# Spreading transfers and moving the weight scaling in a fused attention and mixture-of-experts kernel

## The chip, the core and the metric

The kernel runs on one core of a Trainium2 chip. A core has a matrix engine (TensorE, PE in the rows), a vector engine (VectorE, DVE), a scalar engine (ScalarE, ACT), a general engine (GpSimd, POOL), a queue engine that issues transfers (SyncE, SP), and 16 DMA engines that move data between the device memory, called DRAM in the code, and the on-chip memory. Matmul results land in eight banks of a separate accumulator memory (PSUM). The metric is the device time of one execution in microseconds, the median of three runs.

## What is computed

For each of four batches, 12288 queries of 128 numbers attend to 768 keys. Keys and values are the same rows: a 4x4 mean over `kv`, times `w_sr`. Each attention output goes to one of eight experts, the one with the largest logit, and is scaled by two gates. Softmax and expert choice are per row, so no row waits for another.

```python
kv_pool = kv.reshape(B, H // r, r, W // r, r, C).mean(axis=(2, 4))
k = v = kv_pool.reshape(B, -1, C) @ w_sr
s = scale * (q @ k.transpose(0, 2, 1))
a = softmax(s)
x = a @ v                                   # 49152 rows of 128
e = argmax(x @ w_gate)
out = prob(e) * sigmoid(x @ w_output_gate)[e] * (relu(x @ w1[e]) @ w2[e])
```

## The kernel before

**Tiles.** 512 queries are a group (i, 96 of them, 24 a batch); four groups are a chunk (c, 24 of them). fp32 values are split into a high and a low half of fp16, and a product takes three matmuls (high x high, high x low, low x high). A chunk's most frequent expert is computed in place for all rows of the chunk; rows that chose another expert are written into per-expert lists and done at the end (`tail_tile`).

**Order.** The order of all engines is written out by hand. The outer loop runs over i, the inner one over eight steps s, and a letter string (`ORD`, in the first nine groups `ORDA`) gives the order of the parts in a step: `s` scores of a block of 128 queries (L375 to L379) with the row maximum nm (L381, L382), `h` the first expert product H (L697) with its halves HH (ScalarE, L702) and HL (VectorE, L703), `x` the exponential pr (L396), `r` the rounding of pr to ph (ScalarE L409, then GpSimd subtracts the low half, L410), `u` the product p v (L432: 18 matmuls in a row, at step 5), `y` the second expert product Y (L713 to L715), `e` events put off to a given step, `f` a piece of routing. While group i is at its scores, p v is at i - 1, the logits at i - 2, and the experts at i - 9 (`MOE_LAG`). So the first nine groups do attention alone. ph is transposed by DMA into PT (L415), which p v reads.

**VectorE, ScalarE and GpSimd run their own instructions in order.** A piece that waits holds everything behind it on its engine. H has three PSUM buffers, shared with U of p v.

**Routing.** `routing` (L488 to L603) works in pieces between yields: the sums sume (L499), the one-hot rows, the counts (L524, matmuls hung on the PSUM tile of a score block through `hooks`), the chunk's expert ei (L545), the gate product z (L555), msc, the list places idx (L583), the running list ends (nd and ebase, L586 to L588), and 16 scatters (L599), which wait until the lists are filled.

**Weights.** When the expert is known, `w_load` reads its w1 and w2 (1 MB). `w_split` measures them (L628, two reductions), spreads the two maxima over the rows (wmb L634, a transpose L639, L151 to L157), scales with GpSimd (L666), makes the high half on ScalarE (L673) and the low half on GpSimd (L679). msw (L656) holds the chunk's output factors.

**Transfers on the queue of SyncE.** Queries two groups ahead, keys of the next batch (24 loads of 256 KB, from group 9 of the first batch and group 3 of the others, one a step while at most two blocks are open), list fills (8 of 400 KB, `fill`, from group 9 on), attention values of each group (`u_turn`, a DMA transpose, and `u_out`, the store to `urows`; those of groups 0 to 5 are put off by 48 steps), expert weights and outputs. `kv_prep` sums four rows on GpSimd (L240 to L244), transposes (L248) and multiplies (L211) each of a batch's six key blocks.

Of the kernel before, what the change touches and what calls it, by code (L numbers as in the profile page):

```python
# [53 lines left out]
class Cfg:  # L54
# [8 lines left out]
    ORDA = "hsxruye"  # L63
# [6 lines left out]
    FS = 3  # L70
    HJ = (0, 1)
    H0 = (6, 0)
    LC = 4
    WD = 6
# [6 lines left out]
    UD = 6  # L81
    MT, MO = 4, 2
    KV0, KD = 9, 8
# [4 lines left out]
def body(ctx, tc, q, kv, w_sr, w_gate, w_og, w1, w2, out, cfg=Cfg):  # L88
# [54 lines left out]
    dve.memset(run.rearrange("p (e b) -> p e b", e=E)[:, :, 0:1], 0.0)  # L143
    prow = cst.tile([P, 1], I32, name="prow")
# [35 lines left out]
    KVN = [[0, 0] for _ in range(NB)]  # L180

    def kv_load(b, first=False):

        src = kv[b].rearrange("(ho hl rh) (wq w x) c -> ho w rh hl wq (x c)", ho=3, rh=4, wq=4, w=2)
        for k in range(NKB):
# [13 lines left out]
            for rh in range(4):  # L199
                sp.dma_start(out=halves[rh // 2][:, rh % 2, :], in_=src[k // 2, k % 2, rh])  # L200
                KVN[b][0] += 1
                yield

    def kv_prep(b, fast):
# [13 lines left out]
        for k in range(NKB):  # L218
            while KVN[b][0] < 4 * (k + 1):
# [31 lines left out]
            act.activation(pT, ps[:, 0, 0:P], AF.Copy, scale=1.0 / 16.0)  # L251
            yield
# [59 lines left out]
    def q_power(c, a, b):  # L312

        m, r = (QM[c][:, n, a:b] for n in range(2))
        dve.tensor_scalar(m, m, 2.0 ** -100, 2.0 ** -13, op0=ALU.max, op1=ALU.mult)
# [4 lines left out]
    def q_factor(c, a=0, b=CG):  # L320

        dve.tensor_scalar(QM[c][:, 2, a:b], QM[c][:, 0, a:b], KVT[c // NCH][2], None, op0=ALU.mult)
# [32 lines left out]
    hooks, now = [], [0]  # L355
# [71 lines left out]
    def pv(i, lo, hi, cols=slice(0, GT)):  # L427
# [5 lines left out]
        if hi == len(ops) and cols.stop == GT:  # L433
            u = PVP.pop(i)
            U2 = wk.tile([P, 2, GT], F16, tag="U2", bufs=MOE_LAG, name=f"U2{i}")
# [53 lines left out]
    def routing(c):  # L489
# [9 lines left out]
        dve.tensor_scalar(sume, SUM, vs[:, 0:1], vs[:, 1:2], op0=ALU.mult, op1=ALU.add)  # L499
# [64 lines left out]
        dve.tensor_scalar(sel, m2, cm[:, 1:2], None, op0=ALU.is_equal)  # L564
# [21 lines left out]
        dve.tensor_scalar(nd, w8, cm[:, 1:2], None, op0=ALU.not_equal)  # L586
        dve.tensor_tensor(nd, nd, cnt[:, 0, :], op=ALU.mult)
# [35 lines left out]
    def w_split(c, att):  # L623
        t = WT[c]
        m = kvp.tile([P, 7], F32, tag="wm", name=f"wm{c}")
        mb = kvp.tile([P, 2, P], F32, tag="wmb", bufs=1, name=f"wmb{c}")
        for n in range(2):
            dve.tensor_reduce(out=m[:, n:n + 1], in_=t[:, n, :], op=ALU.max, axis=AX.X,  # L628
                              apply_absolute_value=True)
            if n == 0:  # L630
                yield
                if att and c:
                    yield
        dve.tensor_copy(mb, m[:, 0:2].unsqueeze(2).to_broadcast([P, 2, P]))  # L634
# [7 lines left out]
        if att:  # L642
            hooks.append((now[0] + 2, turn))
        else:
            yield
            yield
# [3 lines left out]
        largest(m[:, 0:2], ps[0][:, :, 384:512])  # L650
# [461 lines left out]
```

## Time and profile before

| | us |
|---|---|
| median of three runs | 2066.92 (2061.56 to 2070.02) |
| profiled execution: its own time | 2066.82 |
| its span, first to last instruction | 2065.1 |
| TensorE busy | 1920.7 (93%) |
| VectorE busy | 1673.5 (81%) |
| GpSimd busy | 1367.5 (66%) |
| ScalarE busy | 1355.9 (66%) |
| mean granted TensorE clock | 0.983 |

The table holds averages over stages that differ: nine groups of attention alone until about 151 us, then groups with experts, with key preparation for the next batch until about 1330 us, and at the end the last expert groups with the lists. A busy share does not say who is late; the waits do. The rows further down are from one profiled execution. Matmuls overlap, so their mean duration is longer than the distance between them.

### The profile page before, as it was taken

The page shows a single profiled execution, that of the slowest core. Times are in us where ns is not written, and L with a number is a line of the kernel's source. Part 1 is how long each engine was busy: PE and PEld are TensorE (multiplying, and loading weights), DVE is VectorE, ACT ScalarE, POOL GpSimd, SP SyncE. Part 2 cuts the span into 40 slices and gives each one's busy share as a digit, 9 for nine tenths or more (in the row PEclk, how much of TensorE's full clock was granted, in tenths as well). Part 3 has the DMA queues.
Part 4 walks back from the last instruction along what each step waited for, and adds up shares of the span by engine and source line. Part 5 has one row for each costly group of instructions (what it writes and reads, how often), then busy time and mean ns, then how long its engine had stood idle before and what let it go on. Part 6 is the DMA issues. An engine that isn't in the chain of part 4 may idle for free.

```text
span 2065.1 us, 31969 instructions
## 1 busy us (share of the span) xinstructions
PE 1920.7 (93%) x10401; PEld 969.2 (47%) x10401; DVE 1673.5 (81%) x3277; ACT 1355.9 (66%) x2501; POOL 1367.5 (66%) x1111
## 2 busy tenths in 40 slices
PE   6878899899999999999999999999999999999996
PEld 4544444444444444444444444444444444444444
DVE  4777688888888888788888888888888888888773
ACT  2656666667677676666766776777777677667542
POOL 2554578788687687675776867856756857757431
PEclk8989999999999999999999999999999999999998
DMA  5959997878988877968889888788788788687411
GB/s 174 184 124 235 199 209 150 180 153 157 203 165 182 197 152 154 176 140 173 163 192 179 186 162 191 136 174 171 138 171 170 146 167 171 141 159 150 100 56 45
DMA packets 902199, 334.10 MB, mean 162 GB/s; under 512 B 820672, under 2 KB 849473, under 8 KB 902032
## 3 DMA queue, kind: packets, MB, share of 16 engines
q1 hardware_dynamic: 889120, 331.59, 77.0%
q0 software_dynamic: 12480, 0.40, 0.5%
q8 instruction: 82, 1.34, 0.3%
q14 instruction: 85, 0.70, 0.1%
q10 hardware_dynamic: 432, 0.07, 0.0%
HBM read 77.80 MB, written 54.53 MB: 64 GB/s over the span
## 4 chain that ended last, share of the span: by engine, by line
DVE 41%; PE 29%; ACT 12%; issue 11%; DMA 4%; POOL 2%; SPq 1%; ACTq 0%; DVEq 0%; POOLq 0%
DVE nm L381 9%; PE U L432 7%; DVE HL L703 7%; ACT pr L396 5%; ACT HH L702 4%; DVE wm L628 2%; PE Y L713 2%; DVE nm L382 2%; PE H L697 2%; PE H L698 2%; PE H L699 2%; PE Y L715 2%; PE Y L714 2%; DVE q L332 2%; DVE U L437 2%
## 5 line engine op out<-in xcount | busy, mean ns | idle before, releaser
L410 POOL TENSOR_TENSOR ph<-pr,ph 128x768 f16<-128x768 f32 x384 | 635.4, 1655 | 486.1 <-ACT ph L409 271.9
L703 DVE SCALAR_TENSOR_TENSOR HL<-H,HH 128x512 f16<-128x512 f32 x768 | 525.2, 685 | 112.6 <-ACT HH L702 102.7
L396 ACT ACTIVATE pr<-S,nm,qm 128x768 f32<-128x768 f32 x384 | 380.3, 990 | 316.8 <-DVE nm L382 287.8
L702 ACT ACTIVATE HH<-H 128x512 f16<-128x512 f32 x768 | 454.2, 592 | 182.4 <-PE H L699 179.3
L599 POOL DMA_INDIRECT scr<-rw,idx x384 | 385.6, 1004 | 97.6 <-issue 87.8
L432 PE MATMUL U<-PT,V 128*128 128x512 f16 (+1 forms) x1872 | 395.3, 366 | 23.2 <-DMA PT<-ph 13.7
L381 DVE TENSOR_REDUCE nm<-S 128x1 f32<-128x768 f32 x384 | 364.1, 948 | 37.5 <-PE S L379 37.3
L697 PE MATMUL H<-U,w 128*128 128x512 f16 x768 | 292.3, 381 | 35.9 <-DVE HL L703 34.1
L409 ACT ACTIVATE ph<-pr 128x768 f16<-128x768 f32 x366 | 307.6, 840 | 7.9 <-DMA PT<-ph 6.0
L713 PE MATMUL Y<-HH,w 128*128 128x512 f16 x768 | 292.9, 381 | 9.2 <-ACT ys L718 9.2
L714 PE MATMUL Y<-HH,w 128*128 128x512 f16 x768 | 291.6, 380 | 1.3 <-POOL w L679 1.3
L699 PE MATMUL H<-U,w 128*128 128x512 f16 x768 | 292.5, 381 | 0.0
L698 PE MATMUL H<-U,w 128*128 128x512 f16 x768 | 292.5, 381 | 0.0
L715 PE MATMUL Y<-HL,w 128*128 128x512 f16 x768 | 291.6, 380 | 0.3 <-DVE HL L703 0.3
L432 PEld LDWEIGHTS <-V 128*128 128x128 f16 x1872 | 184.1, 99 | 222.4 <-issue 25.3
L375 PE MATMUL S<-K,qT 128*128 128x384 f16 x768 | 190.6, 330 | 15.0 <-ACT pr L396 12.4
L379 PE MATMUL S<-K,qT 128*128 128x384 f16 x768 | 191.1, 331 | 0.0
L377 PE MATMUL S<-K,qT 128*128 128x384 f16 x768 | 190.9, 331 | 0.0
L733 DVE TENSOR_TENSOR o<-S,msw 128x256 f32<-128x256 f32 x172 | 73.0, 424 | 101.1 <-ACT pr L396 92.6
L698 PEld LDWEIGHTS <-w 128*128 128x128 f16 x768 | 75.2, 98 | 114.2 <-issue 55.3
L666 POOL TENSOR_SCALAR wr<-wr,wm 128x1024 f32<-128x1024 f32 x44 | 125.1, 2844 | 0.0
L714 PEld LDWEIGHTS <-w 128*128 128x128 f16 x768 | 75.4, 98 | 96.0 <-issue 20.1
(202 smaller groups left out, 2321.3 us busy)
## 6 DMA issues: line engine op xcount, KB each, us to landing
kvs<-in_kv_dram SPq DMA_DIRECT2D x96, 256.0 KB
q<-in_q_dram SPq DMA_DIRECT2D x96, 256.0 KB
wr<-in_moe_w_dram SPq DMA_DIRECT2D x48, 512.0 KB
urows<-uT SPq DMA_DIRECT2D x96, 256.0 KB
out_dram<-o SPq DMA_DIRECT2D x96, 256.0 KB
PT<-ph SPq DMA_TRANSPOSE x384
scr<-rw,idx POOLq DMA_INDIRECT x384
scr<-fill SPq DMA_DIRECT2D x8, 400.0 KB
```

Of the source, the lines that this page charges most:

```text
L381: dve.tensor_reduce(out=nm[:, 0:1], in_=S[:, :, 0:384], op=ALU.max, axis=AX.XY, negate=True)
L396: act.activation(pr.rearrange("p (a k) -> p a k", a=2), S[:, :, 0:384], AF.Exp, bias=nm[:, 1:2], scale=es, accum_out=SUMS[c][:, bl:bl + 1])
L410: pool.tensor_tensor(ph[:, 1, :], pr, ph[:, 0, :], op=ALU.subtract)
L432: pe.matmul(PVP[i][:, cols], ops[n][0], ops[n][1][:, cols], start=(n == 0), stop=(n == len(ops) - 1))
L599: ins = pool.indirect_dma_start(out=scr, out_offset=bass.IndirectOffsetOnAxis(ap=idx[:, bl:bl + 1], axis=0), in_=rw[:, bl, :], in_offset=None,
L697: pe.matmul(H, w1h[:, ts(f, P)], UH, start=True, stop=False)
L698: pe.matmul(H, w1h[:, ts(f, P)], UL, start=False, stop=False)
L699: pe.matmul(H, w1l[:, ts(f, P)], UH, start=False, stop=True)
L702: act.activation(HH, H, AF.Relu)
L703: dve.scalar_tensor_tensor(HL, H, 0.0, HH, op0=ALU.max, op1=ALU.subtract)
L713: pe.matmul(Y, w2h[:, ts(f, P)], HH, start=(f == 0), stop=False)
L714: pe.matmul(Y, w2l[:, ts(f, P)], HH, start=False, stop=False)
```

## The change

1. The list fills are issued once, behind the loads of the first keys and the first three query groups, and the scatters of the first chunks run from group 9 on (`fill`, `routes`).
2. Keys of the next batch: four loads every 16 steps (first batch) or 25 steps (later ones), from group 9 or 2; a block's sums start at the earliest eight steps after its last load; one more step lies between its transpose and its product (`KVP`, `KVD`, `kv_prep`).
3. Value transposes and stores: that of group ri at step 104 + 5 ri, or at its own place where that is later (`UD`, `UDS`). U2, which holds the values until then, has 14 buffers in place of 9.
4. Weights: both reductions and wmb stand at step 5 three steps ahead of the transpose, in front of p v; two `scaled` pieces on ScalarE replace the GpSimd scaling; all pieces have written steps (`WA`, and `WE` for the last two chunks).
5. Small forms on VectorE: sume, sel, msw, wmb, q_power, q_factor and the lower bound in `largest` take a second tensor in place of a number or a single source; nd and its product become one instruction.
6. The count matmuls of the first chunk go to block 2 of group 6 in place of block 0 (`H0`), and a routing piece runs at step 5 in the first nine groups too (`ORDA`).

```diff
-    ORDA = "hsxruye"
+    ORDA = "hsxrfuye"
-    FS = 3
-    H0 = (6, 0)
+    H0 = (6, 2)
-    WD = 6
+    WC = 4
+    WA = ((3, 0, (0, 0)), (4, 0, (3,)), (5, 1, (1, 0, 0), (1, 0, 1), (0, 1)), (6, 0, (2, 0, 0)),
+          (7, 0, (1, 1, 0), (1, 1, 1), (2, 0, 1)), (8, 0, (2, 1, 0)), (9, 0, (2, 1, 1)))
...
-    UD = 6
+    UD, UDS = 13, 5
-    KV0, KD = 9, 8
+    KV0, KVP, KVD = (9, 2), (16, 25), 8
...
-        dve.tensor_scalar(m, m, 2.0 ** -100, None, op0=ALU.max)
+        dve.scalar_tensor_tensor(m, m, 2.0 ** -100, m, op0=ALU.max, op1=ALU.max)
...
+            yield
             keys(k, psA.tile([P, 2, 512], F32, tag="A", name=f"kvk{b}_{k}"), pT)
...
-        dve.tensor_scalar(sume, SUM, vs[:, 0:1], vs[:, 1:2], op0=ALU.mult, op1=ALU.add)
+        dve.scalar_tensor_tensor(sume, SUM, vs[:, 0:1], vs[:, 1:2].to_broadcast([P, CB]), op0=ALU.mult, op1=ALU.add)
...
-        dve.tensor_scalar(nd, w8, cm[:, 1:2], None, op0=ALU.not_equal)
-        dve.tensor_tensor(nd, nd, cnt[:, 0, :], op=ALU.mult)
+        dve.scalar_tensor_tensor(nd, w8, cm[:, 1:2], cnt[:, 0, :], op0=ALU.not_equal, op1=ALU.mult)
...
+        T = 8 * (CG * c + MOE_LAG - 1) - (0 if c else cfg.WC)
+
+        def until(n, middle=False):
+            while now[0] < T + n or middle and not mid[0]:
+                yield
...
+        yield from until(-3, c > 0)
         for n in range(2):
             dve.tensor_reduce(out=m[:, n:n + 1], in_=t[:, n, :], op=ALU.max, axis=AX.X,
                               apply_absolute_value=True)
...
-        dve.tensor_copy(mb, m[:, 0:2].unsqueeze(2).to_broadcast([P, 2, P]))
+        wide = m[:, 0:2].unsqueeze(2).to_broadcast([P, 2, P])
+        dve.tensor_tensor(mb, wide, wide, op=ALU.max)
...
-                pool.tensor_scalar(tn, tn, sc, None, op0=ALU.mult)
...
+        def scaled(n):
+            act.activation(t[:, n, :], t[:, n, :], AF.Copy, scale=m[:, 4 + n:5 + n])
+
+        def high(n, x):
+            act.activation(ws[n][:, 0, ts(x, 512)], t[:, n, ts(x, 512)], AF.Copy)
+
+        def low(n, x):
+            spare["n"] += 1
+            (pool if att else dve).tensor_tensor(ws[n][:, 1, ts(x, 512)], t[:, n, ts(x, 512)],
+                                                 ws[n][:, 0, ts(x, 512)], op=ALU.subtract)
+
+        def factors():
+            MSC[c] = msc = rt.tile([P, CB], F32, tag="msw", bufs=4, name=f"msw{c}")
+            dve.tensor_tensor(msc, MS0.pop(c), m[:, 6:7].to_broadcast([P, CB]), op=ALU.mult)
...
+        drain(fill())
...
-            n = 8 * cfg.UD if ri < cfg.UD else 0
+            n = max(0, 8 * cfg.UD + cfg.UDS * ri - now[0])
...
-                if kp and i % GPB >= k0(i):
-                    next(kl, None)
+                if kp:
+                    n = (8 * (i % GPB - k0(i)) + s) % cfg.KVP[min(i // GPB, 1)]
+                    if n in (0, 2, 4, 6):
+                        next(kl, None)
```

The queue of SyncE at groups 8 and 9, before (PT transposes of ph, uT transposes of values, urows value stores, scr list fills, kvs keys):

```order
L463 DMA_TRANSPOSE uT_1497<-U_508 128x8x128
L463 DMA_TRANSPOSE uT_1499<-U_1387 128x8x128
L415 DMA_TRANSPOSE PT_1399<-ph_2_1511 128x12x128
L415 DMA_TRANSPOSE PT_1399<-ph_3_1538 128x12x128
L301 DMA q_1568<-in_q_dram 128x512
L200 DMA kvs_0_1570<-in_kv_dram 128x1x512
L468 DMA urows<-uT_1497 128x1024
L468 DMA urows<-uT_1499 128x1024
L200 DMA kvs_0_1570<-in_kv_dram 128x1x512
L415 DMA_TRANSPOSE PT_1546<-ph_0_1582 128x12x128
L200 DMA kvs_0_1570<-in_kv_dram 128x1x512
L761 DMA scr<-fill 256x1x400
```

and the same place now:

```order
L423 DMA_TRANSPOSE PT_1410<-ph_2_1523 128x12x128
L423 DMA_TRANSPOSE PT_1410<-ph_3_1550 128x12x128
L309 DMA q_1576<-in_q_dram 128x512
L206 DMA kvs_0_1578<-in_kv_dram 128x1x512
L423 DMA_TRANSPOSE PT_1554<-ph_0_1593 128x12x128
L206 DMA kvs_0_1578<-in_kv_dram 128x1x512
L423 DMA_TRANSPOSE PT_1554<-ph_1_1642 128x12x128
L342 DMA_TRANSPOSE qT_1684<-q_1654 128x8x128
```

The value transposes, their stores and the list fills are gone from this place; the fills stand behind the first query loads, the values further down.

VectorE in the last group of a chunk (i = 79), steps 3 to 6, before (wm is the weights' measure, HL_3 to HL_6 the low halves of H at steps 3 to 6, U the low half of p v's result):

```order
L703 SCALAR_TENSOR_TENSOR HL_3_19449<-H_3_19444,HH_3_19448 128x512
L628 TENSOR_REDUCE wm_19410<-wr_19225 128x1
L634 COPY wmb_19411<-wm_19410 128x256
...
L733 TENSOR_TENSOR o_19465<-S_2_19464,msw_18670 128x256
L332 SCALAR_TENSOR_TENSOR q_19459<-q_18387,qm_18385,q_19459 128x512
L581 TENSOR_REDUCE ix_19496<-x_19441 128x16
L583 SCALAR_TENSOR_TENSOR idx_19498<-sel_19335,ix_19496 128x16
L586 TENSOR_SCALAR nd_19500<-w_94,cm_19191 128x8
L587 TENSOR_TENSOR nd_19500<-nd_19500,cnt_19137 128x8
L588 TENSOR_TENSOR ebase<-ebase,nd_19500 128x8
L703 SCALAR_TENSOR_TENSOR HL_5_19514<-H_5_19509,HH_5_19513 128x512
L437 SCALAR_TENSOR_TENSOR U_19545<-U_19526,U_19545 128x512
```

and the same steps now:

```order
L700 SCALAR_TENSOR_TENSOR HL_3_19432<-H_3_19427,HH_3_19431 128x512
...
L730 TENSOR_TENSOR o_19446<-S_2_19445,msw_18736 128x256
L340 SCALAR_TENSOR_TENSOR q_19442<-q_18374,qm_18372,q_19442 128x512
L589 TENSOR_REDUCE ix_19477<-x_19424 128x16
L591 SCALAR_TENSOR_TENSOR idx_19479<-sel_19321,ix_19477 128x16
L594 SCALAR_TENSOR_TENSOR nd_19481<-w_94,cm_19175,cnt_19118 128x8
L595 TENSOR_TENSOR ebase<-ebase,nd_19481 128x8
L700 SCALAR_TENSOR_TENSOR HL_5_19494<-H_5_19489,HH_5_19493 128x512
L643 TENSOR_REDUCE wm_19244<-wr_19209 128x1 x2
L646 TENSOR_TENSOR wmb_19245<-wm_19244 128x256
L445 SCALAR_TENSOR_TENSOR U_19525<-U_19506,U_19525 128x512
```

Both reductions and wmb went from in front of step 4 to between HL of step 5 and U; nd is one instruction less and stays where it was.

## Rows read from the trace of the kernel before

**Rows 1.** Busy time of each engine in four stretches: the opening without its first 100 us, the body with key preparation, the body without, the end. Columns: stretch in us, its length, busy us and instructions of each engine, granted TensorE clock (1.00 is the full 2.4 GHz), busy share of the DMA engines, GB/s.

```profile
100.00:260.00 160.00, 129.78 (x709) 68.15 (x708) 115.69 (x230) 93.15 (x172) 84.42 (x65) 0.89 0.85 187
260.00:1330.00 1070.00, 1021.66 (x5483) 503.88 (x5482) 907.34 (x1735) 736.11 (x1369) 803.43 (x655) 1.00 0.83 171
1330.00:1900.00 570.00, 559.02 (x3014) 275.82 (x3013) 486.96 (x942) 404.75 (x740) 387.44 (x305) 1.00 0.80 160
1900.00:2066.00 166.00, 139.43 (x723) 70.58 (x721) 103.67 (x238) 73.05 (x129) 50.09 (x52) 0.96 0.29 75
```

**Rows 2.** Waits of TensorE from 100 to 260 us: who waited for whom, us in total, times, the longest.

```profile
PE S L375 <- ACT pr L396: 11.0, 6, 2.5
PE U L432 <- DMA PT<-ph: 5.9, 3, 3.1
PE H L697 <- DVE HL L703: 5.7, 2, 3.9
PE S L524 <- DVE oh L519: 2.3, 1, 2.3
PE S L639 <- DVE qm L322: 2.1, 1, 2.1
PE Y L714 <- POOL w L679: 1.3, 1, 1.3
```

**Rows 3.** The same from 260 to 1900 us.

```profile
PE H L697 <- DVE HL L703: 24.9, 34, 1.9
PE Y L713 <- ACT ys L718: 8.7, 19, 3.0
PE U L432 <- DVE HL L703: 8.0, 15, 0.6
PE kvk L211 <- ACT pT L251: 5.1, 3, 1.9
PE S L730 <- DVE ve L151: 3.0, 2, 1.5
```

**Rows 4.** The same from 1330 to 1900 us, where no keys are prepared.

```profile
PE H L697 <- DVE HL L703: 5.1, 7, 1.0
PE U L432 <- DVE HL L703: 3.7, 7, 0.5
PE Y L713 <- ACT ys L718: 2.0, 7, 0.3
```

**Rows 5.** The DMA queues from 160 to 250 us: queue, packets, MB, share of the 16 engines' time; then what was issued there, times, KB each.

```profile
q1 hardware_dynamic: 46173, 20.91, 102.2%
...
scr<-fill SPq DMA_DIRECT2D x8, 400.0 KB
...
urows<-uT SPq DMA_DIRECT2D x8, 256.0 KB
...
uT<-U SPq DMA_TRANSPOSE x9
```

**Rows 6.** The same queue from 25 to 45 us, while the first keys are made.

```profile
q1 hardware_dynamic: 1568, 0.39, 10.6%
```

**Rows 7.** A wait of VectorE and one of ScalarE from 100 to 260 us, columns as in rows 2.

```profile
DVE o L733 <- DMA out_dram<-o: 8.2, 1, 8.2
...
ACT pr L396 <- POOL ph L410: 8.1, 4, 3.3
```

**Rows 8.** Instructions grouped by line: two of ScalarE and one of GpSimd. Columns: line, engine, operation, out<-in, shapes, count | busy us, mean ns of one | idle before.

```profile
L409 ACT ACTIVATE ph<-pr 128x768 f16<-128x768 f32 x366 | 307.6, 840 | 7.9 <-DMA PT<-ph 6.0 <-issue 1.1 <-ACT HH L702 0.7
...
L673 ACT ACTIVATE w<-wr,wm 128x512 f16<-128x512 f32 x96 | 68.8, 717 | 4.6 <-DVE wm L157 4.6
...
L666 POOL TENSOR_SCALAR wr<-wr,wm 128x1024 f32<-128x1024 f32 x44 | 125.1, 2844 | 0.0
```

**Rows 9.** The same for VectorE.

```profile
L628 DVE TENSOR_REDUCE wm<-wr 128x1 f32<-128x1024 f32 x48 | 57.9, 1209 | 0.0
L499 DVE TENSOR_SCALAR sume<-SUM,ve 128x16 f32<-128x16 f32 x24 | 38.8, 1617 | 0.0
L656 DVE TENSOR_SCALAR msw<-msc,wm 128x16 f32<-128x16 f32 x24 | 34.6, 1441 | 0.0
L555 DVE TENSOR_TENSOR z<-z,rinv 128x16 f32<-128x16 f32 x24 | 30.5, 1270 | 0.8
L586 DVE TENSOR_SCALAR nd<-w,cm 128x8 f32<-128x8 f32 x24 | 29.1, 1211 | 0.0
L634 DVE COPY wmb<-wm 128x256 f32<-128x256 f32 x24 | 16.6, 691 | 0.8
```

**Rows 10.** All engines in order of time in group 75 (i = 75 at its scores), from 1526.1 us on; start and length in us.

```profile
1527.13 0.17 DVE L583 SCALAR_TENSOR_TENSOR idx<-sel,ix 128x16 int32<-128x16 f32 x1
1527.14 1.67 POOL L410 TENSOR_TENSOR ph<-pr,ph 128x768 f16<-128x768 f32 x1 [3.07 <-issue]
1527.22 1.62 DVE L586 TENSOR_SCALAR nd<-w,cm 128x8 f32<-128x8 f32 x1
```

**Rows 11.** TensorE alone at the same place: p v, and the matmul that waits behind it.

```profile
1522.68 4.05 PE L432 MATMUL U<-PT,V 128*128 128x512 f16 x18
...
1529.90 0.38 PE L697 MATMUL H<-U,w 128*128 128x512 f16 x1 [0.68 <-DVE HL L703]
```

More of the change, by code (lines that the diff above doesn't have):

```diff
@@ L143, in body @@
     dve.memset(run.rearrange("p (e b) -> p e b", e=E)[:, :, 0:1], 0.0)
+    c13 = cst.tile([P, CG], F32, name="c13")
+    dve.memset(c13, 2.0 ** -13)
     prow = cst.tile([P, 1], I32, name="prow")
@@ L201, in kv_load @@
                 KVN[b][0] += 1
+                KVI[(b, k)] = now[0]
                 yield
@@ L218, in kv_prep @@
         for k in range(NKB):
-            while KVN[b][0] < 4 * (k + 1):
+            while KVN[b][0] < 4 * (k + 1) or not fast and now[0] < KVI[(b, k)] + cfg.KVD:
                 yield
@@ L353, in q_prep @@
         QS[i] = qT
-    hooks, now = [], [0]
+    hooks, now, mid = [], [0], [False]
     spare = {"n": 0}
@@ L642, in w_split @@
         if att:
-            hooks.append((now[0] + 2, turn))
+            hooks.append((T, turn))
         else:
-            yield
-            yield
+            yield from until(0)
             turn(psA.tile([P, 2, 512], F32, tag="A", name=f"wps{c}"))
@@ L650, in w_split @@
         largest(m[:, 0:2], ps[0][:, :, 384:512])
+        yield from until(2 if att else 0)
         powers(m[:, 2:4], m[:, 4:6], m[:, 0:2])
[L652 removed]
         dve.tensor_tensor(m[:, 6:7], m[:, 2:3], m[:, 3:4], op=ALU.mult)
[L654 to L683 removed]
@@ L684, in w_split @@
-        WT[c] = res
-        for k in range(4 if fast else 8):
-            if k < 4:
-                acts[k]()
-            if k >= 2 and not fast:
-                lows[k - 2]()
-            yield
+        ws = [wk.tile([P, 2, FF], F16, tag=f"w{n}", bufs=2, name=f"w{n}{c}") for n in range(2)]
+        WT[c] = [w[:, h, :] for w in ws for h in range(2)]
+        def scaled(n):
+            act.activation(t[:, n, :], t[:, n, :], AF.Copy, scale=m[:, 4 + n:5 + n])
+        def high(n, x):
+            act.activation(ws[n][:, 0, ts(x, 512)], t[:, n, ts(x, 512)], AF.Copy)
@@ new lines, in low @@
+        def low(n, x):
[5 more added lines that the diff above has]
+            dve.tensor_tensor(msc, MS0.pop(c), m[:, 6:7].to_broadcast([P, CB]), op=ALU.mult)
+        for n, middle, *ops in (cfg.WA if att else cfg.WE):
+            yield from until(n, middle and c)
+            for f, *args in ops:
+                (scaled, high, low, factors)[f](*args)
@@ L909, in body @@
         tix, tgen = [], []
-        filler, begun = None, False
+        begun = False
         def k0(i):
-            return cfg.KV0 if GPB > 20 and i < GPB else 3
+            return cfg.KV0[min(i // GPB, 1)]
         events = {}
@@ L949, in routes @@
             for x in list(rts):
-                if only and x[2] not in SCT:
+                if only and x[2] not in SCT or x[2] in SCT and i < MOE_LAG:
                     continue
@@ L970, in body @@
                 rc = None
-            if i == MOE_LAG:
-                filler = fill()
             for s in range(8):
                 now[0] = 8 * i + s
-                if filler and (8 * i + s) % cfg.FS == 0 and next(filler, 1) == 1:
-                    filler = None
                 if s == 0 and 0 <= ri < NG:
```

60 lines of the change are left out of this document (17 added, 43 removed).

## The prediction

> **What bounds the kernel now.** I read the windows first, one row per stretch of the run [rows 1]. Between 260 and 1900 us TensorE is busy 1021.7 + 559.0 = 1580.7 of 1640 us at full clock, so only 59.3 us are idle there. Between 100 and 260 us it is busy 129.8 of 160 and the granted clock is 0.89. The change gives TensorE no other work, it only moves small transposes, so the time can fall by what TensorE waits, and by the clock. The waits of TensorE by stretch come next: 30.0 us in the 160 us of the opening [rows 2], and some 59 us in the rest of the body [rows 3], most of it for VectorE's HL and ScalarE's ys. Where no keys are prepared any more, 1330 to 1900 us, seven chunks pass in 570 us with 5.1 + 3.7 + 2.0 = 10.8 us of waits, 1.54 us a chunk [rows 4]; 1640 us are then some 20 chunks. So 30.0 + 59.3 us and a clock deficit of 129.8 x 0.11 = 14.3 us are all that can be won before 1900 us. After 1900 us, where TensorE is busy 139.4 of 166, I expect nothing: the last chunks keep their order but for two ScalarE pieces each.
>
> **The change part by part.**
>
> *Lists, value stores.* From 160 to 250 us the DMA queue holds 102% of its engines' time, 20.91 MB [rows 5]. Of that eight list fills are 3.28 MB, eight value stores 2.10 MB, nine value transposes of the same size 2.36 MB: 7.7 MB, 37%. After the change none of the three is in that stretch: the fills stand behind the first keys, where the queue is busy 11% for 20 us [rows 6], and the value stores start at group 13 with one per five steps. 3.28 MB at the 233 GB/s of the full stretch are 14 us, which fits in those 20 us and costs nothing there; if it did not fit, the first p transposes would come up to 14 us late, with the first values due about 10 us after them. With 63% of the bytes the queue is free, and the waits on PT lose their 3.1 us one and about a third of the other 2.8: 4.0 us. The fill also holds one of two buffers of tile o until its last store is out; VectorE waits 8.2 us for a store to free such a buffer [rows 7], TensorE 3.9 us of that behind HL and 2.1 us more at L639, both gone: 6.0 us.
>
> *Counts and weights of the first chunk.* The count matmuls move from group 6, block 0, to block 2, so the 2.3 us wait on oh goes [rows 2]. POOL drops its scaling of the weights, 2844 ns twice a chunk [rows 8]; between groups 7 and 9 that sits in front of ph, and ScalarE's exp waits 8.1 us for POOL ph [rows 7]. Of TensorE's 11.0 us for pr I take the largest two out of six, about 4.5 us, and the 1.3 us for the low weights. On the other side the expert is known later, so VectorE's measure may wait for the weights' load: 0 to 4 us, no such wait exists before; I take 2.
>
> *Clock.* The opening runs at 0.89 while it idles 30 of 160 us; the stretches that idle under 5% run at 1.00 [rows 1]. With over half of the idle time gone I take half of the deficit: 14.3 / 2 = 7.1 us.
>
> Opening: 6.0 + 4.0 + 2.3 + 4.5 + 1.3 + 7.1 - 2 = 23.2 us.
>
> *Two-tensor forms on VectorE.* The small forms are long because of POOL: sume takes 1617 ns, msw 1441, nd 1211, wmb 691 on average [rows 9]. The timeline shows why: nd starts at 1527.22, 0.08 us after POOL's ph subtraction, and ends as that ends, while idx, 0.01 us ahead of POOL, takes 0.17 [rows 10]. A form with two tensors is no cure by itself: z (L555) multiplies two tensors of the same 16 columns and takes 1270 ns [rows 9]. The Trainium skill speaks against the forms too: by its page SBUF — State Buffer, section "Who interferes with whom", a VectorE instruction with two inputs in SBUF contends with a GpSimd instruction that reads SBUF. By that rule the trace agrees for z, and the new forms alone would bring nothing wherever POOL subtracts. What helps by the rows is the place: msw now stands right behind the low part of q and ahead of idx's place in the row, and idx wins there by 0.01 us, so what starts 0.3 us earlier (ix and its gap) wins too. msw's wait then goes, and with it the wait of p v for HL, 3.7 / 7 = 0.53 us a chunk. nd stays where it was and keeps its wait; only one 0.17 us instruction is merged. sume I count at nothing: H, U and Y wait once a chunk each [rows 4], H behind nd and U behind msw, so no wait is left for sume; the work that VectorE has in hand for TensorE hides it, and where that cover is gone it is worth up to its 1617 ns a chunk.
>
> *Weights scaled on ScalarE.* The scaling is two instructions of 128x1024 a chunk. The trace has none. Bounds: above the 840 ns of 128x768 and below two of 717 ns for 128x512 [rows 8], 0.84 to 1.43 us; I take 1.14. The conversions keep their size and leave the place in front of ys, so the 2.0 / 7 = 0.29 us a chunk for ys goes. One scaling lies beside p v, 18 matmuls that take TensorE 4.05 us without a wait [rows 11]; the other stands in front of an HH. Its price lies between 0 (ScalarE is busy 404.75 of 570 us [rows 1]) and 1.14 us a chunk. The nearest row is ys itself, where a conversion of 0.72 us in front costs 0.29: 1.14 / 0.72 x 0.29 = 0.46 us.
>
> *Weights measured beside p v.* Two reductions of 1209 ns and wmb, 3.1 us with its wait, now stand in one piece between HL of step 5 and the low part of U, where before they were a reduction, and a reduction with wmb, some steps earlier. TensorE's wait for HL at that group (0.68 us at 1529.90 [rows 11]) is for the HL ahead of that piece; it can come up to 0.73 us a chunk better, as the earlier pieces are gone, and worse by up to the 3.1 us. I take no change, since the row it is nearest to is p v's 4.05 us, longer than the piece.
>
> Body: 20 x (0.53 + 0.29 - 0.46) = 7.2 us.
>
> *Keys of the next batch.* One more step between the key transpose and its product removes most of the 5.1 us for pT: 4 us. The blocks come every 16 or 25 steps rather than bunched, for which I take half of the 3.0 us for ve, 1.5 [rows 3]. Bounds: 0 to 8.1 us, and below nothing by a wait as long as today's longest for pT, 1.9 us, at each of 18 blocks if POOL's sums now come late; three such waits in the 18 make that unlikely. Keys: 5.5 us.
>
> Sum: 23.2 + 7.2 + 5.5 = 35.9 us. The profiled execution took 2066.8 us (span 2065.1), 0.1 below the median, so the forecast is 2066.8 - 35.9 = 2030.9, 2031 us.
>
> **The rivals.**
>
> *The forms still wait.* msw meets a ph subtraction at its new place, and the 0.53 us a chunk stays: 10.6 us less, 2041.5 us. For it: z with its two tensors, and the 0.01 us by which idx escapes. Against: the 0.3 us of lead. This is also the case in which the change does not do what it says. The Trainium skill's section named above is the rule behind it.
>
> *The opening gains nothing.* The queue was not what held the opening, and the stores, now at 1.6 a group instead of one from group 13 to 31, cost as much as they free. 19 groups x 0.6 x 512 KB at 233 GB/s, 2.2 us each, are 25 us. For it: groups 13 to 31 also take the next keys, and 260 to 1330 us stands at a DMA share of 0.83 [rows 1]. Against: 0.83 leaves 17% free, the addition is some 7%. Time: 2066.8 - 12.7 = 2054 us.
>
> *More than half goes.* If VectorE keeps up everywhere, half of the body's 59.3 us goes, and the other half of the clock's deficit with it: 23.2 + 7.2 + 30 = 60.4 us, 2006 us. For it: HL makes 32.9 of the 59.3 us. Against: nd.
>
> *Slower: the measure's piece delays HL.* The place is step 5 of every fourth group. VectorE is behind TensorE there: nd ends 1.6 us late and HL is late already [rows 10, 11]. If p v is over when VectorE comes to the piece, all 3.1 us fall on the next HL and nm: 20 x 3.1 = 62 us, with 23.2 + 5.5 = 28.7 us still won, which gives 2066.8 + 62 - 28.7 = 2100 us. From a delay of 28.7 / 20 = 1.4 us a chunk on the kernel is slower. Against: the two earlier pieces leave the row, so VectorE arrives earlier by about as much.
>
> **How the numbers follow.** The chances: forecast 0.48 (2013 to 2038 us), forms still wait 0.17, more than half 0.15, opening gains nothing 0.12, slower piece 0.08. The range is 2000 to 2057: it leaves out the slower case, half of the fast one's lower side and the edge of the opening case. About 0.5% (10 us) is what a measurement of this kernel can tell from no change. Faster by more than that, under 2056.6: 0.48 + 0.17 + 0.15 + 0.04 of the opening case = 0.84. Within: 0.07 of the opening case and 0.02 of the slower one = 0.09. Slower: 0.06 and 0.01 = 0.07.
>
> **What would show it.** Windows: between 160 and 250 us a DMA share under 0.8 and a clock above 0.95, and group 13 begun by 230 us. VectorE's o without a wait on a store. Waits: p v on HL and Y on ys near zero after 1330 us, and pr on ScalarE's scaling small; nd still above 1.2 us on average, msw below 0.4. pT under 1.5 us. Wrong would be: H on HL above 1.4 us a chunk, PT waits between groups 13 and 31, or groups of the steady part not shorter by about 0.1 us each.

## The result and the profile after

The changed kernel takes 2010.27 us (median of four runs, 2007.97 to 2013.42) against 2067.24 for the kernel before: a ratio of 0.9729 (95% interval 0.9702 to 0.9755), 57 us less. The forecast was 2031 us, 36 less. The profiled execution has its own time of 2007.97 and a span of 2006.2 us.

The windows of the changed kernel, columns as in [rows 1]:

```profile
100.00:260.00 160.00, 138.54 (x766) 72.75 (x765) 128.19 (x250) 103.91 (x191) 100.68 (x84) 0.91 0.76 150
260.00:1330.00 1070.00, 1042.61 (x5642) 520.15 (x5641) 894.28 (x1763) 782.42 (x1431) 721.51 (x621) 1.00 0.89 181
1330.00:1900.00 570.00, 562.00 (x3052) 279.10 (x3051) 466.65 (x949) 422.91 (x761) 347.03 (x292) 1.00 0.79 156
```

TensorE idles 21.5 of 160 us in the opening where it idled 30.2, and 35.4 of 1640 us behind it where it idled 59.3. Its waits from 260 to 1900 us, the answer to [rows 3]:

```profile
PE H L694 <- ACT lgp L466: 12.2, 16, 1.8
PE S L651 <- DVE qm L330: 6.3, 2, 3.1
...
PE H L694 <- DVE HL L700: 2.9, 4, 0.8
...
PE U L440 <- DVE HL L700: 0.5, 2, 0.2
```

H waited 24.9 us for VectorE's HL, U 8.0: 2.9 and 0.5 are left. Another wait now stands first, that of H behind lgp on ScalarE: 16 times and 12.2 us in all, where it was twice and 1.2 us before. From 100 to 260 us, the answer to [rows 2]:

```profile
PE S L383 <- ACT pr L404: 8.8, 5, 3.0
PE qps L355 <- ACT q L351: 3.9, 2, 2.7
PE S L651 <- ACT pT L258: 3.4, 1, 3.4
```

The waits on PT (5.9 us) and on oh (2.3) are gone and pr has 2.2 us less. That of the query transposes (qps) was 1.1 us and is 3.9, and one for the new keys' pT has come up.

Where the time went is read most surely from the place of a group: the first score matmul of group 14 and of group 95 in the timeline, first of the kernel before, then of the changed one.

```profile
273.14 0.80 PE L375 MATMUL S<-K,qT 128*128 128x384 f16 x2
...
1906.31 0.49 PE L375 MATMUL S<-K,qT 128*128 128x384 f16 x2
```

```profile
256.01 0.48 PE L383 MATMUL S<-K,qT 128*128 128x384 f16 x2
...
1855.14 0.49 PE L383 MATMUL S<-K,qT 128*128 128x384 f16 x2
```

Group 14 comes 17.1 us earlier, the 81 groups from there to group 95 take 1599.1 us in place of 1633.2 (34.1 less), and from group 95 to the end of the span it is 151.1 in place of 158.8 (7.7 less). The table below gives the same three stretches for every experiment.

### The profile page after: what moved, and what is told of

It is laid out like the page before. It is cut to its first block, busy times and chain, and to the rows that moved or that the text cites. A ratio compares the mean times of both kernels' runs of the same rounds, so it can differ in the third digit from the quotient of the medians.

```text
span 2006.2 us, 31998 instructions
## 1 busy us (share of the span) xinstructions
PE 1903.0 (95%) x10401; PEld 970.8 (48%) x10401; DVE 1612.4 (80%) x3254; ACT 1403.2 (70%) x2549; POOL 1240.1 (62%) x1067
## 4 chain that ended last, share of the span: by engine, by line
PE 55%; DVE 23%; ACT 8%; issue 8%; DMA 4%; POOL 1%; SPq 0%; DVEq 0%; ACTq 0%; POOLq 0%
PE U L440 11%; PE Y L710 5%; PE H L694 5%; DVE nm L389 5%; PE H L696 5%; PE H L695 5%; PE Y L711 5%; PE Y L712 5%; PE S L387 4%; PE S L385 4%; PE S L383 4%; DVE HL L700 3%; ACT pr L404 3%; DVE wm L643 2%; ACT HH L699 2%
## 5 line engine op out<-in xcount | busy, mean ns | idle before, releaser
L445 DVE SCALAR_TENSOR_TENSOR U<-U,U 128x512 f16<-128x512 f32 x96 | 66.2, 689 | 73.4 <-ACT U L444 68.7
```

## The experiments

Eleven edits and the changed kernel once more were profiled and timed, each against the kernel before in the same session. In the first two sessions the kernel before took 2081 and 2083 us, in the third 2066.8 (2067.24 beside the result), so ratios are compared, not times; for the changed kernel itself they were 0.9729 and 0.9761, so a difference of some 0.3% across sessions says nothing. The three stretches of each profile are in us: from the start of group 2 to that of group 14, from there to that of group 95, and from there to the end of the span.

| kernel | session | 2 to 14 | 14 to 95 | 95 to end | ratio to before (interval) |
|---|---|---|---|---|---|
| before | | 215.6 | 1633.2 | 158.8 | 1 |
| changed | | 200.8 | 1599.1 | 151.1 | 0.9729 (0.9702 to 0.9755) |
| changed, again | 2 | 204.0 | 1600.0 | 173.1 | 0.9761 (0.9741 to 0.9780) |
| e1 forms back | 1 | 200.4 | 1599.6 | 173.6 | 0.9779 (0.9749 to 0.9808) |
| e2 GpSimd scales | 1 | 205.8 | 1661.1 | 173.9 | 1.0094 (1.0063 to 1.0125) |
| e3 measure back | 1 | 200.2 | 1600.2 | 171.0 | 0.9773 (0.9743 to 0.9803) |
| e4 fill back | 1 | 198.5 | 1596.8 | 174.5 | 0.9762 (0.9734 to 0.9790) |
| e5 stores back | 2 | 203.6 | 1598.5 | 173.6 | 0.9759 (0.9739 to 0.9778) |
| e7 keys back | 2 | 196.0 | 1593.3 | 172.4 | 0.9695 (0.9677 to 0.9713) |
| e9 weights back | 2 | 210.7 | 1637.0 | 173.2 | 0.9983 (0.9968 to 0.9998) |
| e11 weights alone | 3 | 208.3 | 1586.3 | 151.8 | 0.9711 (0.9692 to 0.9729) |
| e14 ScalarE scales, alone | 3 | 205.9 | 1637.5 | 159.8 | 0.9992 (0.9982 to 1.0001) |
| e6 fill and stores back | 3 | 207.3 | 1594.9 | 151.1 | 0.9744 (0.9723 to 0.9765) |
| e15 key loads back | 3 | 196.8 | 1585.6 | 151.4 | 0.9663 (0.9643 to 0.9683) |

Two profiles of the changed kernel differ by 3.3 us in the first column and by 0.9 in the second: that is the measure for the rest, though a spread taken from two profiles is itself rough.

### The changed kernel again

> The changed kernel itself, beside the others on one chip, so that the end of the run (after the scores of group 95) can be compared. If the 20 us more that the first four experiments spend after group 95 belong to their edits, this run ends 151 us after the scores of group 95 begin (as the changed kernel did before); if they belong to the chip they ran on, the end varies with the chip and the start of group 95 stays at 1855 us within 2.

It ended 173.1 us after the start of group 95, which stood at 1862.0, 7 us late; 2.7 of these arose ahead of group 2, 3.3 up to group 14 and 0.9 behind it. So the 20 us at the end that e1 to e4 also show belong to the session and not to their edits (sessions 1 and 3 bear the same chip number on record, so the chip does not explain it either), and the second column can be compared across sessions, the third only within one. That the start of group 95 would stay within 2 us was a miss.

### e1: the small forms as before

```diff
-        dve.scalar_tensor_tensor(sume, SUM, vs[:, 0:1], vs[:, 1:2].to_broadcast([P, CB]), op0=ALU.mult, op1=ALU.add)
+        dve.tensor_scalar(sume, SUM, vs[:, 0:1], vs[:, 1:2], op0=ALU.mult, op1=ALU.add)
...
-            dve.tensor_tensor(msc, MS0.pop(c), m[:, 6:7].to_broadcast([P, CB]), op=ALU.mult)
+            dve.tensor_scalar(msc, MS0.pop(c), m[:, 6:7], None, op0=ALU.mult)
...
```

> The changed kernel (2010 us) with part 5 undone: sume, sel, msw, wmb, nd, q_power, q_factor and the lower bound in largest in the forms of before. Theory A (the form decides how long VectorE waits, and that time is what TensorE no longer waits for): sume back from 0.58 to about 1.6 us and msw from 0.26 to over 1 us, TensorE's waits for HL between 260 and 1900 us up from 4 to 15 us or more, time 2022 to 2035 us. Theory B (the places decide, the forms are incidental): msw stays under 0.5 us in its new place, the waits for HL stay under 8 us, time 2006 to 2015 us.

Theory B holds, by the stretches and the ratio. VectorE's groups in the changed kernel, then in e1 (columns as in [rows 9]):

```profile
L594 DVE SCALAR_TENSOR_TENSOR nd<-w,cm,cnt 128x8 f32<-128x8 f32 x24 | 24.7, 1031 | 0.0
L507 DVE SCALAR_TENSOR_TENSOR sume<-SUM,ve 128x16 f32<-128x16 f32 x24 | 13.9, 580 | 0.0
L646 DVE TENSOR_TENSOR wmb<-wm 128x256 f32<-128x256 f32 x24 | 11.3, 472 | 0.8
L681 DVE TENSOR_TENSOR msw<-msc,wm 128x16 f32<-128x16 f32 x24 | 6.2, 257 | 0.0
```

```profile
L594 DVE TENSOR_SCALAR nd<-w,cm 128x8 f32<-128x8 f32 x24 | 24.9, 1036 | 0.0
L507 DVE TENSOR_SCALAR sume<-SUM,ve 128x16 f32<-128x16 f32 x24 | 13.8, 573 | 0.0
L646 DVE COPY wmb<-wm 128x256 f32<-128x256 f32 x24 | 7.8, 325 | 0.8
L681 DVE TENSOR_SCALAR msw<-msc,wm 128x16 f32<-128x16 f32 x24 | 7.6, 318 | 0.0
```

sume fell from 1617 ns to 580 with the new form and to 573 with the old one; wmb as a copy is even shorter. The stretch from group 14 to 95 is the same to 0.5 us, and the ratio is not told apart from the changed kernel's (0.9779 and 0.9761, intervals overlapping). The 2034.5 us of this run lie outside the 2006 to 2015 that theory B named, by the session's longer last stretch.

### e9: the weights as before, the forms new

Part 4 is undone as a whole (the old `w_split` and its calls), with msw and wmb in their new forms.

> The changed kernel with part 4 undone: measure in two pieces, GpSimd's scaling in the chain of its own, no pieces at written steps, msw at its old place; small forms stay new. Theory I (the plan of the weights as a whole, and not the forms, gives most of the body's 34 us): from group 14 to group 95 1615 us or more instead of 1599.1, HL's waits from 260 to 1900 us 20 us or more, msw over 1 us again. Rival (the forms with the old plan are enough, either alone takes VectorE out of the way): within 6 us of 1599.1.

Theory I holds: 1637.0 us from group 14 to 95, no less than the kernel before, and a ratio of 0.9983. sume and msw, new forms and old places:

```profile
L507 DVE SCALAR_TENSOR_TENSOR sume<-SUM,ve 128x16 f32<-128x16 f32 x24 | 37.6, 1567 | 0.0
...
L664 DVE TENSOR_TENSOR msw<-msc,wm 128x16 f32<-128x16 f32 x24 | 31.4, 1306 | 0.0
```

Why is read in the timeline (start, length). First the new form in e9, then the old form in e1, in a chunk of the steady part:

```profile
1556.65 1.04 POOL L606 DMA_INDIRECT scr<-rw,idx  x1 [0.15 <-issue]
1557.36 2.07 DVE L507 SCALAR_TENSOR_TENSOR sume<-SUM,ve 128x16 f32<-128x16 f32 x1
1557.73 1.66 POOL L418 TENSOR_TENSOR ph<-pr,ph 128x768 f16<-128x768 f32 x1
```

```profile
1515.70 0.31 DVE L507 TENSOR_SCALAR sume<-SUM,ve 128x16 f32<-128x16 f32 x1
1515.80 0.99 POOL L607 DMA_INDIRECT scr<-rw,idx  x1 [0.15 <-issue]
...
1516.82 1.66 POOL L418 TENSOR_TENSOR ph<-pr,ph 128x768 f16<-128x768 f32 x1
```

In e9 sume starts 0.7 us into GpSimd's scatter and ends 0.04 us after the ph subtraction behind it; in e1 it starts 0.1 us before the scatter and is through long before the subtraction. For sume the form does not matter, the 0.8 us by which GpSimd and VectorE stand otherwise do.

### e11: the weights' plan alone

The kernel before with part 4. The edit also leaves out, as the changed kernel does, the routing piece at step 5 in the last group of each chunk (`if i % CG != 3: routes(1)`), which the list of parts does not name; e9 puts it back. So where these two speak of the weights' plan, this piece is in it, and no run separates it.

> The kernel before with part 4 alone (the plan of the weights; forms, lists, stores and keys as before). Theory I (the plan is what gives the body): from the start of group 14 to that of group 95 1592 to 1602 us instead of 1633.2, group 14 at 262 to 266 us instead of 273, the time 35 to 50 us under the kernel before on the same chip, and sume under 0.7 us in its old form. Rival (the plan needs the other parts, which clear its way): less than 20 us under the kernel before.

Theory I holds and is short of the mark: 61 us under the kernel before (0.9711), as fast as the whole change within the intervals, with the old forms, lists, stores and keys. Each stretch has its share, -7.3, -46.9 and -7.0 us, and their sum is the 61.1 us of the times to 0.1. Its waits from 260 to 1900 us:

```profile
PE kvk L215 <- ACT pT L255: 7.8, 8, 2.2
PE H L690 <- ACT lgp L462: 6.4, 10, 0.7
PE H L690 <- DVE HL L696: 4.4, 6, 1.0
```

HL is nearly gone (24.9 us before), as in the changed kernel, and pT still has its wait, of which the changed kernel has got rid. Yet the changed kernel takes 12.8 us longer from group 14 to 95: parts 1 to 3, 5 and 6 cost there what they win in the opening (7.5 us, 4.3 by the second profile), and more. Where no keys are prepared, four chunks from group 76 to 92 take 308.9 us here and 308.6 in the changed kernel (315.4 before, 314.9 in e9), so there the plan is the whole gain.

### e14: ScalarE scales, alone

```diff
-                pool.tensor_scalar(tn, tn, sc, None, op0=ALU.mult)
+                act.activation(tn, tn, AF.Copy, scale=sc)
```

> The kernel before with one edit: the scaling of the weights by ScalarE in place of GpSimd, at the same place in the old chain. Theory C (GpSimd's 2.84 us twice a chunk are what the plan saves): group 14 to group 95 in 1615 us or less instead of 1633.2, sume and msw a third shorter. Theory B (the places of the pieces on VectorE and GpSimd are what the plan saves): within 6 us of 1633.2, sume over 1.4 us, the waits of Y for ys longer as ScalarE's scaling stands in front of it.

Theory B holds for the time: 1637.5 us from group 14 to 95, a ratio of 0.9992. msw keeps its 1431 ns, while sume, at its old place and in its old form, falls to 678 ns: 21 of its 24 now begin about 1 us into a ph subtraction and wait for the rest of it alone. So 1 us less of sume bought nothing here, as the forecast had it. The waits for ys are the 8.7 us of [rows 3] and no longer, where theory B had them longer. The opening is 9.7 us shorter (205.9 against 215.6), as much as with the whole plan, the body 4.3 longer. From 260 to 1900 us a new wait appears, the transpose of the logits behind HL:

```profile
PE H L697 <- DVE HL L703: 18.2, 28, 1.2
PE lT L476 <- DVE HL L703: 9.8, 13, 0.8
```

### e2: GpSimd scales at the new steps

```diff
-            act.activation(t[:, n, :], t[:, n, :], AF.Copy, scale=m[:, 4 + n:5 + n])
+                pool.tensor_scalar(t[:, n, :], t[:, n, :], m[:, 4 + n:5 + n], None, op0=ALU.mult)
```

> The changed kernel with the scaling of the weights by GpSimd (2.84 us, twice a chunk) in place of ScalarE (two pieces), at the same steps. Theory A (GpSimd had room, the swap between engines brings little in the body): within 6 us of 2010 us, sume and msw under 0.8 us. Theory C (GpSimd's load is what held ph, the forms on VectorE and with them HL): 2020 us or more, ScalarE's waits on GpSimd's ph and VectorE's mean forms longer by a third. Theory D (the scaling on ScalarE is what makes TensorE wait for lgp, 12.2 us between 260 and 1900 us): faster, 2000 us, with those waits halved.

Nearest to theory C, but not by its mechanism: 1.0094, and 62 us more from group 14 to 95, with sume at 772 ns. The wait is a new one:

```profile
PE H L700 <- POOL w L680: 39.9, 20, 3.7
```

20 times H waits for the low half of the next chunk's weights. In this edit ScalarE's conversion waits for GpSimd's scaling (40.7 us in all), which in the kernel before it did not (it scaled for itself), so the whole chain comes late. The waits for lgp stay at 12.0 us, so theory D falls. With e14 this says: ScalarE's scaling is no gain by itself over the whole run, but the written steps cannot be kept without it.

### e3: the measure at its old places

```diff
-        yield from until(-3, c > 0)
+        yield from until(-7 if c else -3)
         for n in range(2):
+            if n and c:
+                yield from until(-5)
```

> The changed kernel with the measure of the weights from chunk 1 on back in two pieces at steps 1 and 3 of the same group, in front of the stretch where HL was late, in place of one piece at step 5 beside p v. Theory B (the place of these 2.8 us is what made VectorE arrive in time for HL): TensorE's waits for HL between 260 and 1900 us rise from 4 to 15 us or more, U's with them, time 2022 us or more. Theory A (the forms' saving is enough): the waits for HL stay under 8 us, time within 6 us of 2010 us.

A split answer. The waits for HL rose as theory B says, the time did not, as theory A says:

```profile
PE H L696 <- DVE HL L702: 16.5, 19, 2.1
...
PE H L696 <- ACT lgp L466: 1.8, 1, 1.8
```

HL has 13.6 us more and lgp 10.4 less: as I read it, where VectorE comes later at one group, TensorE arrives later at the next, and the wait for lgp there is absorbed. The measure beside p v is worth about 1 us in all (1600.2 against 1599.1), no more than two profiles of one kernel differ by, as long as the other pieces stand where they now do; the four chunks from group 76 to 92 take 309.1 us against 308.6.

### e4, e5, e6: lists and stores

e4 issues the fills from group 9 on again, e5 takes the old rule for the stores, e6 does both.

```diff
-            n = max(0, 8 * cfg.UD + cfg.UDS * ri - now[0])
+            n = 48 if ri < 6 else 0
```

> The changed kernel with the list fills back at group 9, one every third step. Theory E (the fill's bytes and its buffer of tile o held the opening): group 13 starts 6 us later or more, VectorE waits over 5 us for a store to free an o buffer, the waits on PT return with 2 us or more, time 2017 to 2025 us. Theory F (the opening is held by ScalarE and VectorE, and the value stores were the excess): time within 4 us of 2010 us.

> The changed kernel with part 3 undone: the transposes and stores of the values at their own places, those of groups 0 to 5 put off by 48 steps. Theory G (the value stores in groups 9 to 13 held the opening): group 14 begins at 262 us or later instead of 256.0, and group 95 as much later; time 2016 to 2024 us, waits on PT from 100 to 260 us of 2 us or more. Theory F (the opening was held by the order of the first chunk, not by bytes): group 14 within 2 us of 256.0.

> The changed kernel with parts 1 and 3 both undone: list fills at group 9 and value stores at their own places. Theory K (either of the two clears the queue enough, both together are what filled it): group 14 begins 5 us or more later after group 2 than in the changed kernel (200.8 us), the waits on PT from 100 to 260 us over 3 us, VectorE waits over 5 us for a store to free an o buffer. Theory F (the bytes never held the opening): within 3 us of 200.8, the time within 6 us of the changed kernel on this chip.

Alone neither costs anything: 198.5 and 203.6 us from group 2 to 14, against 200.8 and 204.0 in two profiles of the changed kernel, and ratios of 0.9762 and 0.9759 against 0.9761. Theories E and G fall. Both together take 6.5 us more there than the first profile of the changed kernel and 3.3 more than the second, fill the queue again and bring the PT wait back. The queue from 160 to 250 us in the changed kernel and in e6, then a wait of TensorE and one of VectorE in e6 from 100 to 260 us (first fence: changed):

```profile
q1 hardware_dynamic: 35267, 13.39, 74.1%
```

```profile
q1 hardware_dynamic: 46279, 20.03, 101.5%
...
PE U L440 <- DMA PT<-ph: 3.0, 1, 3.0
...
DVE o L730 <- ACT HH L699: 9.2, 1, 9.2
```

Theory K, then, by its waits; the 5 us that it named hold against the first profile alone. VectorE's wait for an o buffer comes back too: the profile puts the 9.2 us down to HH, but the store of the earlier o, issued at 211.1 us, lands at 216.14, this o starts at 216.23, and the HH that ends at 216.20 is of no use to it. It is the place of the 8.2 us in [rows 7]; the changed kernel has no such wait. Alone the fills leave the queue at 88.1% and the stores at 94.0%. But e6's time, 0.9744, is not told apart from the changed kernel's 0.9729: from group 14 to 95 e6 is 4.2 us shorter.

### e7, e15: the keys

e7 undoes part 2, e15 only the spread of the loads. This cut is in both; both also begin a later batch's loads at its group 3 again instead of 2, and e7 further drops the eight steps ahead of the sums and the step ahead of the product, and holds key preparation to certain steps of a chunk, as before:

```diff
-                if kp:
-                    n = (8 * (i % GPB - k0(i)) + s) % cfg.KVP[min(i // GPB, 1)]
-                    if n in (0, 2, 4, 6):
-                        next(kl, None)
+                if kp and i % GPB >= k0(i):
+                    next(kl, None)
```

> The changed kernel with part 2 undone: one key load a step, sums as soon as a block is loaded, and the product one step behind the transpose. Theory H (the keys' spread gave 5.5 us as forecast): from the start of group 14 to that of group 95 1604.6 us instead of 1599.1, waits on pT of 4 us or more. Rival (nothing, or worse now: their waits only change place): within 3 us of 1599.1, the waits on pT instead of those of S on qm.

> The changed kernel with the loads of the next keys back to one a step (from group 9 or 3 on), but with the later sums and the longer way from transpose to product kept. Theory L (the spread of the loads over the batch is what costs the 14 us): as fast as the kernel with part 2 undone, a ratio to the kernel before of 0.967 to 0.972. Theory M (the later sums and the longer way are what costs): as the changed kernel, 0.974 or more.

e7 is faster than the changed kernel: 0.9695 against 0.9761 in one session, 14.2 us, 6.8 of them from group 14 to 95. Both of its theories fall. e15 is faster still: 0.9663 (0.9643 to 0.9683), 1995.04 us, 72 us under the kernel before and the fastest of all. Theory L's cause holds, and its mark (0.967 to 0.972) is passed: the spread of the loads costs some 15 us, 13.5 of them from group 14 to 95, as much as the changed kernel loses there against e11. The later sums, the longer way to the product and the freedom to prepare keys at any step, which e15 has and e7 hasn't, win 7.6 us together from group 14 to 95 (1585.6 against 1593.3), and with them goes e7's wait:

```profile
PE kvk L218 <- ACT pT L258: 6.7, 6, 2.1
```

Where the spread costs is read group by group against e15: groups 31 and 32 take 3.2 us more, 55 and 56 the same, groups 46 and 70 3.1 us each; the other groups differ by up to 3.7 us both ways, 0.9 us in sum, and the opening takes 4.0 us more, hardly above the spread of two profiles. In group 55 of the changed kernel, in order of time:

```profile
1084.72 1.64 POOL L418 TENSOR_TENSOR ph<-pr,ph 128x768 f16<-128x768 f32 x1 [1.61 <-ACT ph L417]
1084.76 1.63 DVE L591 SCALAR_TENSOR_TENSOR idx<-sel,ix 128x16 int32<-128x16 f32 x1
...
1087.25 2.33 DVE L643 TENSOR_REDUCE wm<-wr 128x1 f32<-128x1024 f32 x2
...
1089.47 0.27 PE L255 MATMUL kvt<-ident,kvs 128*128 128x128 f32 x1
...
1092.97 0.42 DVE L730 TENSOR_TENSOR o<-S,msw 128x256 f32<-128x256 f32 x1 [0.61 <-ACT pr L404]
1093.31 0.15 DVE L330 TENSOR_TENSOR qm<-qm,ve 128x4 f32<-128x4 f32 x1
...
1093.54 0.41 PE L651 MATMUL S<-ident,wmb 128*128 128x128 f32 x2 [3.14 <-DVE qm L330]
```

idx, ahead of GpSimd by 0.01 us in [rows 10], is 0.04 us behind it here and takes 1.63 us; the measure follows, VectorE reaches o and qm late, and TensorE waits 3.1 us. That lateness is not the whole cause, though: in e15 VectorE is as late in this group (ebase, two instructions on, is held for 1.50 us there, and from the o before these to qm it takes 9.7 us against 9.9), and TensorE does not wait. What e15 does not have at this place is kvt, the transpose of the new keys; its own stands 12.7 us earlier in the group. By the code kvt takes one of the two PSUM buffers that the score blocks share, so that, as I read it, the next block has to wait for the buffer of the block before, which o has read at 1093.39. Right behind the wait, from 1093.9 to 1097.3 us, the granted clock is 0.50 (1.2 GHz), where e15 has 1.00 throughout from group 14 to 95. In group 70 the last steps of the new keys stand on VectorE behind U's low part, and three waits for HL in a row are 3.1 us (1.2, 0.9 and 1.0 by the distance of the matmuls).

## Why the forecast was right, and by how much it was not

Faster, within the range (2000 to 2057), but 57 us in place of 36, and nearer to the rival *more than half goes* (2006). That the time came into the range is in part luck. The weights' plan alone gives the whole gain (e11, 0.9711 against 0.9729), and the forecast had it at 7.2 us in the body and, its clock aside, some 4 in the opening. Of the lists, the stores and the keys it expected 15.5 us; in the kernel as changed they bring nothing over the plan, since the spread of the key loads costs what the other parts bring. With that spread undone (e15) they bring 10.6 us.

**The ceiling was read too low.** I took TensorE's idle time, 59.3 us, for all that the body holds. From 1500 to 1850 us the two windows are, before and after:

```profile
1500.00:1850.00 350.00, 342.92 (x1844) 169.32 (x1843) 301.16 (x581) 246.07 (x450) 229.69 (x183) 1.00 0.80 162
```

```profile
1500.00:1850.00 350.00, 347.71 (x1891) 173.13 (x1889) 286.36 (x577) 263.87 (x474) 222.13 (x185) 1.00 0.81 160
```

TensorE's idle time fell by 4.8 us of 350, 1.4%, but it did 47 matmuls more, 2.5%. From the start of group 14 to that of group 95 its idle time fell from 57.0 to 35.0 us, 22.0 of the 34.1 us won; the other 12.1 came out of its busy time (1576.2 to 1564.2), with 8476 and 8479 matmuls and a granted clock of 1.00. Matmuls overlap, those of H being 0.38 us long and 0.21 apart, so that one behind a wait shows longer than the step it costs, and a part of the wait is counted as busy. Four chunks from group 76 to group 92 took 315.4 us and take 308.6: 1.7 us a chunk, more than the whole 1.54 us of waits in [rows 4].

**The body: too little.** Forecast 7.2 + 5.5 = 12.7 us, measured 34.1 from group 14 to 95, and 46.9 for the plan without the spread keys (e11). The mechanism, VectorE in time for HL, stood in the text: msw from in front of U's wait (0.53), the conversions from in front of ys (0.29), the two pieces of the measure out of HL's way (up to 0.73). I gave the last no value, and charged 0.46 for ScalarE's scaling. With 0.73 and no price the sum is 1.55 us a chunk, near the 1.7, but that is worked out afterwards, and for the 0.73 e3 speaks against it. The row on ScalarE:

```profile
L669 ACT ACTIVATE wr<-wr,wm 128x1024 f32<-128x1024 f32 x48 | 55.2, 1150 | 2.1 <-DVE wm L162 2.1
```

Its duration was forecast (1.14), its price was not there: the conversions behind it fell from 717 ns to 633, and ScalarE was busy 422.9 of 570 us. With the measure back (e3) the waits move and the time stays: four chunks take 309.1 us, 0.1 us a chunk more, not 0.73. The plan counts as a whole (e9, e11). Which of msw's place, the conversions' places and the routing piece left out at step 5 does most of it no run has separated.

**The forms** are no cure, the place is: right (e1, e9), and with it the rival *the forms still wait* falls, since msw takes 257 ns at its new place. The Trainium skill's page SBUF — State Buffer, section "Who interferes with whom", speaks against two inputs in SBUF; here the old form of sume, with a single tensor, waits just as long where it stands badly (1617 ns on average [rows 9], 1567 for the new one in e9), which fits that section's other sentence, that copies and tensor_scalar can contend as well under conditions it refers to; whether sume met them no run here shows. nd keeps its wait: right, at 1.03 us instead of over 1.2.

**The keys** were a miss in sign: 5.5 us forecast, of which 4 for the longer way and 1.5 for the spread. The longer way and the later sums, with the freedom of the step, gave 7.6, the spread took some 15 us. I weighed when blocks come against each other, not what they meet: as I read the groups above, blocks spread over the batch meet the groups in which VectorE is just in time, and there their transposes take a buffer of the scores and their last steps stand in front of HL.

**The opening**: forecast 23.2, measured 17.1 to the start of group 14 (14.8 from group 2 on, 11.6 by the second profile). The weights' plan alone gives 7.3 of it, and the scaling taken off GpSimd as much by itself (9.7 in e14), for which I had 4.5 + 1.3. Fills and stores gave 3.3 to 6.5, for which I had 10; each of the two suffices, since either leaves the queue enough. The 6.0 of these for the o buffer were too much: in e6 VectorE's wait is back in full (9.2 us), and TensorE waits 3.2 us for HL where the changed kernel waits 2.4. The fills themselves fit behind the first keys, as forecast: group 2 begins at 55.3 us, before at 57.6. Group 13 begins at 236.6 us (249.0 before), not by 230. The clock rose from 0.89 to 0.91: 138.5 x 0.09 = 12.5 us of deficit in place of 14.3, 1.8 us won and not 7.1, because the stretch from 100 to 160 us kept its 0.83 (from 160 to 260 us 0.93 became 0.97). In the second profile of the changed kernel the two have 0.86 and 0.95, so this part is not sure to a us or two. The part that H0 and `ORDA` have was not tried alone; e6, which has them, and e11, which hasn't, are 1.0 us apart, less than two profiles of one kernel.

**The end**: forecast none, measured 7.7 us. It goes with the plan (151.8 us in e11, 159.8 in e14): by the distance of its matmuls TensorE in the kernel before waits 1.7 and 1.8 us for HL at 1930.6 and 1933.3, while VectorE makes the low weights of the last chunk but one in a row. By its idle time it also waits 1.2 us for HL in front of p v at 1918.5 and 1.9 us at 1972.7, where the transpose of the last chunk's measure waits for VectorE's list work; e14 has all four, e11 and the changed kernel none. The timeline of that piece before, and in the changed kernel, where the pieces have written steps (`WE`) and no such wait follows:

```profile
1929.19 0.75 DVE L675 SCALAR_TENSOR_TENSOR w<-wr,wm,w 128x512 f16<-128x512 f32 x1 [0.19 <-ACT w L673]
1931.01 1.63 DVE L675 SCALAR_TENSOR_TENSOR w<-wr,wm,w 128x512 f16<-128x512 f32 x1 [0.47 <-ACT w L673]
1933.17 0.73 DVE L675 SCALAR_TENSOR_TENSOR w<-wr,wm,w 128x512 f16<-128x512 f32 x1
```

```profile
1880.00 0.68 DVE L676 TENSOR_TENSOR w<-wr,w 128x512 f16<-128x512 f32 x1
1881.52 0.68 DVE L676 TENSOR_TENSOR w<-wr,w 128x512 f16<-128x512 f32 x1
...
1884.39 0.68 DVE L676 TENSOR_TENSOR w<-wr,w 128x512 f16<-128x512 f32 x1
```

**The rivals.** *More than half goes* had the body's mechanism right (VectorE in time) and the clock wrong. *The slower piece* is real in the two groups where the measure and new keys meet, 2 x 3.1 us, not in 20 chunks. *The opening gains nothing* was half right: the stores' bytes did not have to go as long as the fills had.

## What to carry to other kernels

Count the distance between matmuls or groups, not TensorE's idle time, when you set the ceiling of a gain. Where an engine is a little late in one group of four, price a piece by who waits behind its old place, not by its duration, and expect a wait that is undone to reappear elsewhere. Before background work is spread evenly, look up what it meets in each period: here four loads every 25 steps cost some 15 us more than one load a step.

## What was not expected of the hardware

A VectorE form's length beside GpSimd depends on tens of nanoseconds: idx took 0.17 us when it began 0.01 us before GpSimd's subtraction [rows 10] and 1.63 us when it began 0.04 us after it. In all of the changed kernel 14 of the 24 idx begin 5 to 9 ns before such a subtraction and take 174 to 176 ns, and three begin 46 ns after its start and take 1.63 us. In two of the three sessions of experiments every kernel that was profiled spent some 20 us more behind group 95 (173 us against 151 in the changed kernel itself); in e1 ScalarE then stands up to 5.1 us in front of single instructions without a releaser that the profile names, and what holds it stayed open.
